# A transformer block on one core: fewer maxima made ahead, another order of token tiles, and where the last transposition stands

## The chip, the cores and the metric

One core of a Trainium2 chip runs the whole program. The metric is the device time of an execution in microseconds (us); the kernel before was run three times, and one further execution was recorded by the profiler.

## The reference

A pre-LayerNorm transformer block in fp32, 2048 tokens, model width 576, 32 heads of 18, and a gated MLP of width 4608. Scale and softmax over all keys, without a mask; LayerNorm without weights.

```python
h  = x + MHA(layernorm(x)) @ wo          # q, k, v = layernorm(x) @ wqkv, 32 heads, Dh = 18
p  = softmax(q @ k.T * Dh**-0.5)         # per head, 2048 x 2048
h2 = h + (gelu(layernorm(h) @ w_gate) * (layernorm(h) @ w_up)) @ w_down
```

The kernel reaches fp32 accuracy by splitting each operand into a high and a low fp16 part.

## The kernel before, in words

**Stages.** (1) LayerNorm, and the products for q, k and v. (2) Attention in 32 blocks `n`: 8 groups of four heads (`g`) times 4 blocks of 512 queries (`qc`); each block runs over 16 tiles of 128 keys (`kt`), one tile a step. (3) The product with wo, token tile by token tile (16 tiles of 128 tokens), with the residual and the statistics of the second LayerNorm. (4) The MLP (line 1246 and on), whose normed rows and their sums are prepared by `rows0` and `rows1`.

**Maxima.** The softmax of a block needs the maximum of each row of scores before its scores are exponentiated. The generator `maxima` makes them: for each block 64 calls of `max_bank`, each four small matmuls (54 rows x 32 columns, a column group each, line 674) into one PSUM bank, and a reduction on DVE (line 687). In one of eight calls ("over") ACT takes the bank instead (line 681), and the last of the eight ("both", line 685) adds this in. A call for head `h` uses the row half `h % 2` of the PE array: rows 0 to 63 or 64 to 127. In each run of eight the heads come as 0, 1, 1, 3, 3, 2, 2, 0.

`max_finish` ends a block: DVE reduces the 64 columns (L698), POOL makes the high and low halves (L701 to L703), SP transposes them by DMA (L705, `mT<-mm`) and copies four parts of `mT` into rows of the query stacks Q (L711, `W<-mT` or `A<-mT`). The first score of the block needs these rows.

**Ahead and beside.** 98 calls of the maxima are made during stage 1, four at a time between the half products of q, k and v (the loop over `i`, line 1369), the rest in the steps of stage 2, eight a pair of steps ("m" in `STEPS`). So the maxima run ahead by 98 calls, and a block's `max_finish` falls into step `kt` = 7 of the block before it. In a step, "S" and "s" are scores and their exponentials on ACT, "w" is `weigh` (the product with V, L765), "f" takes a portion of side work, mostly POOL's: `prepare_wo` in block 2, `split_early` (line 1160) and the sums of `split_matrix` (L1114) from block 28 to 30.

**Late steps.** The maxima end 24 steps before the end of stage 2 (`LAST_MAX`). From there the steps follow `LATE`: in place of the maxima each takes "L", a half token tile of the product with wo (14 matmuls of 288 columns, L335, added to x on DVE at L908). `wo_pairs` goes over tiles 0, 4, 1, 5, 2, 6, 3, 7, then `wo_block(2)` over tiles 8 to 11: 24 halves. After the second tile of each pair POOL makes the reciprocal deviations (`rstd_beside`) of both, and `rows0`, taken in portions by `rows_at`, makes the rows for the MLP, transposed by SP (L996).

**Block outputs.** `out_block(n)` has three parts: in the next block's first step the sums are copied out (L776, L777) and the denominators sent round by DMA (L780); at `kt` = 3 come the reciprocals (POOL L787, DVE L793 from block 28 on; L795, L798); at `kt` = 9 the product (POOL L801 to L803; DVE L805 to L807 from block 29 on), and the copies of the block's rows into X (L822, L826 `X<-nat`) on SP's and POOL's queues. Blocks 28 to 31 are the last head group of the four query blocks, so tokens 0 to 511 (tiles 0 to 3) need block 28's rows, and tiles 4 to 7 block 29's. Block 29's third part comes at `kt` = 8 of block 30, by the exception in line 1413.

**Order.** The instructions of each engine, SP's queue included, stand in the order of the program: what waits holds up what is behind it on the same engine. At the step with `after` == -1 (the last with maxima: `n` = 30, `kt` = 7) SP also gets the load of x tiles 5 to 7 (L1421) and two loads for `wo_block(2)` (L897).

After the loop come `weigh` of the last half, what is left of `fill` (nothing), and the second half; then the MLP.

Of the kernel before, what the change touches and what calls it, by code (L numbers as in the profile page):

```python
# [32 lines left out]
def tile_block(  # L33
# [23 lines left out]
    NT = S // P  # L57
    TB = min(512, S)
    NB = S // TB
    TPB = TB // P  # L60
# [67 lines left out]
    def view(region, off, shape, dtype=None):  # L128

        dtype = dtype or region.dtype  # L130
        v = region if dtype == region.dtype else region.bitcast(dtype)
        size = 4 if dtype == F32 else 2
        n = math.prod(shape)
        assert off % size == 0
        v = v[:, off // size : off // size + n]
        if len(shape) == 2:
            v = v.rearrange("p (a b) -> p a b", b=shape[1])
        elif len(shape) == 3:
            v = v.rearrange("p (a b c) -> p a b c", b=shape[1], c=shape[2])
        return v  # L140
# [188 lines left out]
    def accumulate(dst, pairs, bank=None):  # L329

        xs = []
        for i, (a, b) in enumerate(pairs):
            if i == len(pairs) // 2:
                yield
            m_ = nc.tensor.matmul(dst, a, b, start=(i == 0), stop=(i == len(pairs) - 1))  # L335
            if isinstance(bank, int):
                xs.append(of_triple(m_, (bank,), True))
        if xs:
            wrote((bank,), xs)

    def run(it):
        for _ in it:
            pass
# [8 lines left out]
    def take(it, n=1):  # L352
        for _ in range(n):
            next(it, None)
# [340 lines left out]
    def max_finish(n, mx):  # L695
        g, qc = divmod(n, NB)
        m = small.tile([P, 4, TPB], F32, tag="m", name="m")
        nc.vector.tensor_reduce(m, mx.rearrange("p t h c -> p h t c"), axis=AX.X, op=ALU.max)  # L698
        mm = mms[n % 2]
        hst = mm[:, : 8 * TPB].rearrange("p (h s t) -> p h s t", h=4, s=2)  # L700
        nc.gpsimd.tensor_scalar_mul(m, m, 1 / MSC)  # L701
        nc.gpsimd.tensor_copy(hst[:, :, 0], m)
        nc.gpsimd.tensor_sub(hst[:, :, 1], m, hst[:, :, 0])  # L703
        mT = small.tile([P, 1, P], F16, tag="mT", name="mT")
        nc.sync.dma_start_transpose(mT, mm)  # L705
        for pr in range(2):
            Q = sets[g % 2][pr][0]
            for j in range(2):
                k = (4 * pr + 2 * j) * TPB
                row = 64 * j + R1  # L710
                nc.sync.dma_start(Q[row : row + 2, qc * TB : (qc + 1) * TB],  # L711
                                  mT[k : k + 2 * TPB, 0])
# [117 lines left out]
    NS = NG * NB  # L830
    UPS = TPB * NB
    AHEAD = UPS + 8 * UPS // 16
# [3 lines left out]
    def maxima():  # L836

        for n in range(NS):
            mx = small.tile([P, TPB, 4, NB], F32, tag="mx", name="mx")
            over, both = ("over", "both") if n else ("one", "one")  # L840
            if n:
                nc.gpsimd.memset(mx[:, :, 0, 1::2], LOWEST)
            for u in range(0, UPS, 2):
                t, k = divmod(u, NB)
                for unit in ((over, t, k + 1, 0), ("one", t, k, 1), ("one", t, k + 1, 1), ("one", t, k, 3),
                             ("one", t, k + 1, 3), ("one", t, k, 2), ("one", t, k + 1, 2), (both, t, k, 0)):
                    max_bank(n, mx, *unit, bank=bank_now[0])
                    yield
            max_finish(n, mx)

    oh = view(W, 6 * 2 * S, (NK + 1, D))
    ol = view(W, 6 * 2 * S + 2 * (NK + 1) * D, (NK + 1, D))
# [33 lines left out]
    xbs = [view(A, MAT, (D,)), view(WK, 19968, (D,))]  # L886
# [3 lines left out]

    def wo_tiles(ts, ring_, xbs=xbs):

        by = ts[1] - ts[0]

        def fetch(k):
            if xbs and k < len(ts):
                nc.sync.dma_start(xbs[k % 2], xv[:, ts[k]])  # L897

        fetch(0)
        fetch(1)  # L900
        yield
        for k, t in enumerate(ts):
            for i in range(2):
                ws = slice(i * HALF, (i + 1) * HALF)
                pt = next(ring_)
                run(accumulate(pt[:, :HALF], products(slice(t * P, (t + 1) * P), oh, ol, ws)))
                of_x = xbs[k % 2] if xbs else nat[:, t]
                nc.vector.scalar_tensor_tensor(nat[:, t, ws], pt[:, :HALF], u_o, of_x[:, ws],  # L908
                                               op0=ALU.mult, op1=ALU.add)
                if i == 1:  # L910
                    fetch(k + 2)
                    row_stats(nat[:, t], t)
                    if k % 2:
                        rstd_beside(t - by, 2, 256.0, by)
                        rows_made.update((t - by, t))
                yield
# [4 lines left out]

    def wo_pairs(ring_):

        return wo_tiles([t for i in range(TPB) for t in (i, TPB + i)], ring_, None)


    VP = view(V, 0, (2 * PIECES, TB), F16)
# [428 lines left out]
    mxs = maxima()  # L1356
# [10 lines left out]
    side = iter(())  # L1367
    take(fill, 19)
    for i in range(5 * AHEAD // 4):
        take(mxs, 0 if i % 5 == 4 else 6 if i == 5 * AHEAD // 4 - 2 else 4)  # L1370
        if i == AHEAD // 4:
            raw_loads()
        take(fill, 2 + (i % 6 == 2))
        if i >= AHEAD // 3:
            take(sums)
        if i == 5 * AHEAD // 4 - 6:
            nc.scalar.activation(root, eps, AF.Exp)
            scale_wo()
# [3 lines left out]
    STEPS = [step.split() for step in ("m4 S010 w m2 s25 m3 w s34 f", "m0 S011 m5 w s34 s23 m0 w m5 m2 f")]  # L1382
    halves = deque([None, None])
    LATE = "S010 s22 s33 w L w f".split()
    LAST_MAX = (NS - 1) * NT - 8
    rows_at = {4 * (i + 1) + k: c for i in range(TPB) for k, c in ((1, 2), (3, 3), (4, 3))}
    rows = rows0()
    in_order.enter_context(tc.manual_schedule(engines={EngineType.SP}))
    loads = iter(())
    for n in range(NS):  # L1390
        g, qc = divmod(n, NB)
        late = n > NS - NB
        for kt in range(NT):
            after = n * NT + kt - LAST_MAX
            for step in LATE if after >= 0 else STEPS[kt % 2]:
                if step[0] in "sS":
                    score(n, kt, [int(c) for c in step[1:-1]], int(step[-1]))
                elif step[0] == "m":
                    bank_now[0] = int(step[1])
                    take(mxs)  # L1400
                elif step == "L":
                    take(fill)
                elif step == "w":
                    half_ = halves.popleft()
                    if half_ is not None:
                        weigh(*half_)
                        if half_[1] == NT - 1 and half_[3] == 1:
                            ob = out_block(half_[0], accs)
                            next(ob)
                else:  # L1410
                    take(side)
            halves += [(n, kt, accs, q) for q in range(2)]
            if n and kt in (2 if n == NS - 1 else 3, {NS - 1: 5, NS - 2: 8}.get(n, 9)):
                take(ob)
            if 8 <= n < 13 and kt == 14:
                nc.sync.dma_start(nat[:, n - 8], xv[:, n - 8])
            if after == -1:
                wo_ring = ring([singles[1], quad])
                fill, third = wo_pairs(wo_ring), wo_block(2, wo_ring)
                take(fill)  # L1420
                nc.sync.dma_start(nat[:, 5:8], xv[:, 5:8])  # L1421
                take(third)
                fill = chain(fill, third)
            take(rows, rows_at.get(after, 0))
            if g == 0 and qc == 0 and kt == NT - 1:
                run(fill)
                init_set(sets[1])
            if g + 1 < NG and (qc, kt) == ((1, 2) if g == 0 else (0, 10)):
                loads = load_group(g + 1)
            take(loads)  # L1430
            if g + 1 < NG and qc == 1 and kt == 10:
                steps_made = key_steps(g + 1)
                take(steps_made)
            if g + 1 < NG and qc == 1 and kt == 13:
                run(steps_made)
            if n == 2 and kt == 4:
                side = prepare_wo()
            if n == NS - NB and kt == 0:
                blank_rows()
                loads = matrix_loads(w_gate, 0, nc.gpsimd)  # L1440
                take(loads)
            if n == NS - NB and kt == 2:
                run(loads)
                side = chain(split_early(0, 0, lambda: load_matrix(w_up, 0, nc.gpsimd)), pause(2),
                             split_early(0, 1, lambda: load_matrix(w_gate, 1, nc.gpsimd)),
                             pause(2), until_ready(second))
# [55 lines left out]
    for sc in range(NCH // 2):  # L1502
        c = 2 * sc
# [52 lines left out]
```

## Time and profile before

| | us |
|---|---|
| median of three runs | 2581.53 (2581.3 to 2583.08) |
| the profiled execution | 2580.42 |
| its span, first to last instruction | 2578.6 |
| PE busy | 2545.7 (99%) |
| DVE busy | 1990.8 (77%) |
| ACT busy | 1654.7 (64%) |
| POOL busy | 913.8 (35%) |
| first matmul of the maxima | 103.78 |
| first score | 208.95 |
| end of the maxima (last L698) | 1276.56 |
| MLP begins | 1370.07 |

The rows of the profile have these forms. A timeline row: start in us, duration in us, engine, line, operation, output<-input with shapes, xcount for merged neighbours, and in brackets the idle time before it and what ended it. A row of the chain: start, duration, engine, tile, line. A row of the waits: who waited, for whom, total us, times, longest. A row of stretches: from:to, length, then busy time (and instructions) of PE, PEld, DVE, ACT, POOL, the granted clock of PE, the share of the DMA engines, GB/s. PE is TensorE's matmuls, PEld its weight loads, SPq SP's DMA queue. A busy PE is not PE at its peak.

### The profile page before, as it was taken

The numbers are of one execution on the slowest core, as the hardware profiler recorded it, in microseconds if no ns is written. First come the engines' busy times: TensorE is split into PE (matmuls) and PEld (weight loads), VectorE is DVE, ScalarE is ACT, GpSimd is POOL, SyncE is SP. The second block draws the span as 40 slices with busy tenths as digits, with TensorE's granted clock in tenths as the row PEclk, the third lists the DMA queues.
The fourth block names the chain that finished last, engine by engine and source line by source line (L and its number), as shares of the span: only waits on it lengthen the run. The fifth ranks groups of instructions, "written<-read, shape, count | busy, mean of one in ns | idle before, by whom it ended". The sixth has DMA issues, their size and how long they took to land.

```text
span 2578.6 us, 95994 instructions
## 1 busy us (share of the span) xinstructions
PE 2545.7 (99%) x41245; PEld 1472.2 (57%) x41245; DVE 1990.8 (77%) x3891; ACT 1654.7 (64%) x2723; POOL 913.8 (35%) x1299
## 2 busy tenths in 40 slices
PE   8999999999999999999989999999999999999999
PEld 4645555555555555555555555555555555555555
DVE  7478999999999999999856674757575756565653
ACT  7437999999999999999855433334343424333332
POOL 4301644343434343446846332323231323232221
PEclk9999999999999999999999999999999999999999
DMA  8620111021202010111133410101010101010110
GB/s 220 155 72 28 48 37 33 17 59 28 52 19 49 21 46 21 41 25 30 39 80 90 93 44 14 51 12 52 13 35 30 34 30 35 30 34 30 35 56 37
DMA packets 177601, 120.98 MB, mean 47 GB/s; under 512 B 94188, under 2 KB 154548, under 8 KB 177174
## 3 DMA queue, kind: packets, MB, share of 16 engines
q1 hardware_dynamic: 163378, 95.92, 14.0%
q0 software_dynamic: 13664, 18.91, 3.0%
q8 instruction: 322, 5.28, 0.9%
q14 instruction: 105, 0.86, 0.1%
q10 hardware_dynamic: 132, 0.01, 0.0%
HBM read 80.05 MB, written 15.01 MB: 37 GB/s over the span
## 4 chain that ended last, share of the span: by engine, by line
PE 74%; DVE 18%; issue 5%; POOL 2%; DMA 1%; ACT 1%; SPq 0%; DVEq 0%; ACTq 0%; POOLq 0%
PE more L1246 15%; PE bank L1246 15%; DVE mx L687 13%; PE bank L335 10%; PE bank L765 9%; PE more L335 8%; PE triple L674 4%; DVE nat L685 3%; PE bank L674 3%; PE triple L742 2%; PE triple L335 2%; PE bank L742 2%; PE quad L335 2%; PE quad L674 1%; DMA A<-qk_hi 0%
## 5 line engine op out<-in xcount | busy, mean ns | idle before, releaser
L765 PE MATMUL bank<-WK,V 64*32 64x256 f32 x16384 | 761.1, 379 | 0.1
L751 ACT ACTIVATE WK<-triple 128x1024 f32<-128x1024 f32 x512 | 539.9, 1054 | 43.7 <-PE triple L742 42.3
L687 DVE TENSOR_REDUCE mx<-triple 128x1 f32<-128x512 f32 x731 | 499.6, 683 | 1.1 <-PE quad L674 0.3
L753 ACT ACTIVATE WK<-bank 128x512 f32<-128x512 f32 x756 | 434.1, 617 | 3.7 <-PE bank L742 0.3
L687 DVE TENSOR_REDUCE mx<-bank 128x1 f32<-128x512 f32 x577 | 387.4, 680 | 23.1 <-PE bank L674 22.2
L1246 PEld LDWEIGHTS <-W 128*128 128x128 f16 x2394 | 234.2, 98 | 278.4 <-issue 0.2
L335 PEld LDWEIGHTS <-WK 128*128 128x128 f16 x3456 | 338.2, 98 | 88.3
L765 PEld LDWEIGHTS bank<-WK,V 64*32 64x32 f32 x16384 | 351.0, 106 | 44.8 <-DVE nat L777 7.6
L674 PEld LDWEIGHTS <-W 54*32 54x32 f16 x4096 | 143.1, 89 | 169.9 <-issue 107.1
L335 PE MATMUL more<-W,WK 128*128 128x288 f16 x1728 | 235.2, 286 | 0.0
L335 PE MATMUL bank<-W,WK 128*128 128x288 f16 x1728 | 235.2, 286 | 0.0
L674 PEld LDWEIGHTS <-A 54*32 54x32 f16 x4096 | 136.8, 89 | 169.1 <-issue 109.0
L787 POOL TENSOR_TENSOR rp<-rc,minus_one 128x4 f32<-128x4 f32 x112 | 111.6, 1010 | 339.3 <-DMA rc<-nat 339.3
L1246 PE MATMUL more<-X,W 128*128 128x512 f16 x792 | 223.8, 379 | 0.0
L1114 POOL TENSOR_TENSOR A<-A 128x384 f32<-128x384 f32 x136 | 138.9, 1042 | 199.6 <-DMA A<-in_B_w_up_dram 115.2
L674 PE MATMUL triple<-W 54*32 54x512 f16 x2048 | 203.0, 384 | 2.8 <-DVE mx L687 1.3
L1246 PE MATMUL more<-V,W 128*128 128x512 f16 x720 | 202.4, 379 | 0.0
L1260 POOL TENSOR_TENSOR WK<-tmp,WK 128x512 f16<-128x512 f32 x73 | 88.2, 1208 | 308.0 <-ACT WK L1257 307.9
L674 PE MATMUL triple<-A 54*32 54x512 f16 x1852 | 184.2, 385 | 2.0 <-ACT WK L751 0.5
L685 DVE CUSTOM_DVE_ANT_0 nat<-triple,nat 128x512 f32<-128x512 f32 x244 | 165.6, 679 | 0.9 <-PE triple L674 0.9
L687 DVE TENSOR_REDUCE mx<-quad 128x1 f32<-128x512 f32 x244 | 165.7, 679 | 0.2 <-PE quad L674 0.2
L1264 ACT COPY tmp<-bank 128x512 f32<-128x512 f32 x36 | 21.0, 583 | 222.3 <-PE bank L1246 220.7
(363 smaller groups left out, 4676.5 us busy)
## 6 DMA issues: line engine op xcount, KB each, us to landing
A<-in_B_w_down_dram SPq DMA_DIRECT2D x8, 1152.0 KB
nat<-rc SPq DMA_DIRECT2D x128, 64.0 KB
A<-in_B_w_gate_dram SPq DMA_DIRECT2D x64, 128.0 KB
A<-in_B_w_up_dram SPq DMA_DIRECT2D x64, 128.0 KB
qk_hi<-tmp SPq DMA_DIRECT2D x36, 128.0 KB
qk_lo<-tmp SPq DMA_DIRECT2D x36, 128.0 KB
out_dram<-nat SPq DMA_DIRECT2D x16, 288.0 KB
nat<-in_A_x_dram SPq DMA_DIRECT2D x3, 1152.0 KB
```

The source lines that it names most:

```text
L335: m_ = nc.tensor.matmul(dst, a, b, start=(i == 0), stop=(i == len(pairs) - 1))
L674: mm = [nc.tensor.matmul(pm[c : c + CT, :TB], Q[r, q0 + c : q0 + c + CT], keys, start=True, stop=True) for c in range(0, P, CT)]
L685: x_ = nc.vector.tensor_tensor_reduce(row, pm[:, :TB], row, 1.0, LOWEST, ALU.add, ALU.max, dst)
L687: x_ = nc.vector.tensor_reduce(dst, pm[:, :TB], axis=AX.X, op=ALU.max)
L742: mm.append(nc.tensor.matmul(pS[c : c + CT, :TB], K[r, k0 : k0 + CT], Q[r, qc * TB : (qc + 1) * TB], start=True, stop=True))
L751: act = nc.scalar.activation(pe, triple[:, bank : bank + 2], AF.Exp, scale=ex_reg)
L753: act = nc.scalar.activation(pe[:, heads[0] % 2], bank_at(bank)[:, :TB], AF.Exp, scale=ex_reg)
L765: nc.tensor.matmul(acc[CT * c : CT * c + CT, :QH], Vg[n // NB][ks, v : v + CT], pes[(2 * kt + q) % NPE][ks, j, qh * QH : (qh + 1) * QH], s ...
L787: nc.gpsimd.tensor_tensor(rc[:, c : c + 4], den[:, c : c + 4], minus_one.to_broadcast([P, 4]), op=ALU.pow)
L1114: op(W8[:, d], W8[:, a], W8[:, b])
L1246: nc.tensor.matmul(bank, w, x_, start=start and i == 0, stop=i == len(mm) - 1, skip_group_check=not start)
L1260: nc.gpsimd.tensor_sub(hl[:, 2 * i + j], v, hh[:, 2 * i + j])
```

## The change

- Of the maxima, 90 calls instead of 98 are made in stage 1: four at a time up to `i` = 26, two at 27, none at 28 and 29. In these the heads of a run of eight come as 0, 1, 1, 2, 3, 2, 3, 0, so that the row halves alternate.
- So every `max_finish` falls two steps later, into `kt` = 9 of the block before, ahead of that step's third part of `out_block`. The maxima end two steps later, at `n` = 30, `kt` = 9; there are 22 late steps, and two half tiles (tile 11) are taken by `run(fill)` between the two last calls of `weigh`.
- For the last block, `max_finish` pauses eight times between POOL's part and the transposition. Block 29's third part moves from `kt` = 8 to 9, the same step, and `run(mxs)` issues the last transposition and its four copies behind it.
- The token tiles come as 0, 1, 4, 5, 2, 6, 3, 7; `rstd_beside` is called after each tile from 4 on; the steps at which `rows0` is taken follow.

```diff
@@ max_finish
         nc.gpsimd.tensor_sub(hst[:, :, 1], m, hst[:, :, 0])
+        if n == NS - 1:
+            yield from [None] * 8
         mT = small.tile([P, 1, P], F16, tag="mT", name="mT")
@@ maxima
-                for unit in ((over, t, k + 1, 0), ("one", t, k, 1), ("one", t, k + 1, 1), ("one", t, k, 3),
-                             ("one", t, k + 1, 3), ("one", t, k, 2), ("one", t, k + 1, 2), (both, t, k, 0)):
+                order = ((over, k + 1, 0), ("one", k, 1), ("one", k + 1, 1), ("one", k, 3),
+                         ("one", k + 1, 3), ("one", k, 2), ("one", k + 1, 2), (both, k, 0))
+                for kind, kc, h in [order[i] for i in (0, 1, 2, 5, 3, 6, 4, 7)] if n * UPS + u < AHEAD - 2 else order:
+                    unit = kind, t, kc, h
                     max_bank(n, mx, *unit, bank=bank_now[0])
                     yield
-            max_finish(n, mx)
+            yield from max_finish(n, mx)
@@ wo_tiles
-        by = ts[1] - ts[0]
+        by = 1 if xbs else TPB
...
-                    if k % 2:
+                    if k % 2 if xbs else t >= TPB:
                         rstd_beside(t - by, 2, 256.0, by)
@@ wo_pairs
-        return wo_tiles([t for i in range(TPB) for t in (i, TPB + i)], ring_, None)
+        return wo_tiles([0, 1, TPB, TPB + 1, 2, TPB + 2, 3, TPB + 3], ring_, None)
@@ stage 1
     for i in range(5 * AHEAD // 4):
-        take(mxs, 0 if i % 5 == 4 else 6 if i == 5 * AHEAD // 4 - 2 else 4)
+        take(mxs, 0 if i % 5 == 4 else 4 if i < 27 else 2 if i == 27 else 0)
@@ stage 2
-    LAST_MAX = (NS - 1) * NT - 8
-    rows_at = {4 * (i + 1) + k: c for i in range(TPB) for k, c in ((1, 2), (3, 3), (4, 3))}
+    LAST_MAX = (NS - 1) * NT - 6
+    rows_at = {7: 2, 8: 3, 9: 3, 10: 2, 11: 3, 12: 3, 13: 2, 15: 3, 16: 3, 17: 2, 19: 3, 20: 3}
...
-            if n and kt in (2 if n == NS - 1 else 3, {NS - 1: 5, NS - 2: 8}.get(n, 9)):
+            if n and kt in (2 if n == NS - 1 else 3, {NS - 1: 5, NS - 2: 9}.get(n, 9)):
                 take(ob)
+            if after == -1:
+                run(mxs)
```

## The prediction

> **What bounds the kernel now.** I read first the page, then the busy times in stretches, then the chain of waits and the timelines around the one stretch in which TensorE is idle.
>
> ```profile
> span 2578.6 us, 95994 instructions
> PE 2545.7 (99%) x41245; PEld 1472.2 (57%) x41245; DVE 1990.8 (77%) x3891; ACT 1654.7 (64%) x2723; POOL 913.8 (35%) x1299
> ```
>
> TensorE is bound nearly everywhere, so a gain must be idle PE time, or PE work. The stretches (us; busy time of each engine; granted clock; DMA share; GB/s):
>
> ```profile
> 107.30:143.30 36.00, 36.00 (x383) 22.46 (x383) 28.63 (x50) 20.43 (x68) 10.91 (x16) 1.00 0.55 129
> 143.30:196.40 53.10, 52.81 (x378) 21.66 (x375) 40.71 (x78) 12.09 (x21) 1.48 (x5) 1.00 0.25 82
> 216.07:1276.50 1060.43, 1055.66 (x31092) 614.05 (x31078) 1056.60 (x2014) 1056.43 (x1731) 470.02 (x750) 1.00 0.14 35
> 1283.08:1302.66 19.58, 9.09 (x133) 4.76 (x125) 2.19 (x8) 4.00 (x6) 0.92 (x2) 0.65 0.27 86
> 1320.92:1368.68 47.76, 47.76 (x891) 30.38 (x896) 32.80 (x87) 28.73 (x44) 29.44 (x59) 1.00 0.62 118
> ```
>
> Before 196 us (maxima beside products) PE is full and DVE is not. In the long middle, with maxima in every step, DVE is as full as PE. In the late steps PE alone is full, except from 1283 to 1303, where it works 9.09 of 19.58 us. Who it waits for there (engine, line, releaser: us, times, longest), and the SP queue at that place:
>
> ```profile
> PE bank L335 <- DMA X<-nat: 10.5, 1, 10.5
> ```
> ```profile
> 1282.56 1.12 SPq L705 DMA_TRANSPOSE mT<-mm  x1
> 1285.51 2.70 SPq L711 DMA_DIRECT2D W<-mT  x4
> ...
> 1289.81 5.07 SPq L822 DMA_DIRECT2D X<-nat  x6
> ```
>
> The second token tile of the order 0, 4, 1, 5 needs block 29's rows (X<-nat). The copies are issued last, behind the last transposition, its four copies and loads of x (lines 1421 and 897, between the two). The transposition itself was late; the chain has POOL's sums of a weight matrix before it:
>
> ```profile
> 1277.75 2.91 POOL A L1114 x3
> ```
>
> It also gives the last copy of rows before PE goes on, issue included, and what a late step costs:
>
> ```profile
> 1293.26 2.51 DMA X<-nat
> ```
> ```profile
> 1302.86 0.41 PE triple L742 x12
> 1303.30 0.43 PE bank L765 x16
> 1303.73 1.82 PE bank L335 x14
> ```
> ```profile
> 1307.01 1.82 PE quad L335 x14
> ```
>
> A late step is 3.28 us (1303.73 to 1307.01), 1.82 of it the half token tile. The stretch 1283.08 to 1302.66 holds two steps and took 19.58, so the stall costs 19.58 - 2 x 3.28 = 13.0 us: 10.5 of waiting, the rest slow matmuls at the lower clock.
>
> **The change, part by part.**
>
> *The stall: tile order (edits of `wo_tiles` and `wo_pairs`), rows ahead of the transposition (the pause in `max_finish`, `run(mxs)` after `take(ob)`).* DVE around the place, with two marks one pair of steps apart:
>
> ```profile
> 1271.48 0.68 DVE L685 CUSTOM_DVE_ANT_0 nat<-triple,nat 128x512 f32<-128x512 f32 x1
> 1275.76 0.68 DVE L685 CUSTOM_DVE_ANT_0 nat<-triple,nat 128x512 f32<-128x512 f32 x1
> 1276.56 0.22 DVE L698 TENSOR_REDUCE m<-mx 128x16 f32<-128x64 f32 x1
> 1279.97 1.24 DVE L805 TENSOR_TENSOR nat<-nat 128x512 f32<-128x512 f32 x1
> 1281.76 0.69 DVE L807 TENSOR_TENSOR nat<-nat 128x512 f16<-128x512 f32 x1
> ```
>
> A pair of steps with maxima is 4.28 us. Two more such steps put the last L698 and the start of the late steps at 1276.5 + 4.3 = 1280.8 (on the time scale of before). L805 to L807 (2.5 us) then follow L698 at once: rows ready at 1283.5. SP is free (its next work is theirs) and issues six copies in 5.07: 1288.6; the last lands at 1287.8 + 2.51 = 1290.3. POOL's own two copies follow the POOL sums of the maxima, which now start with L698, since POOL's backlog L1114 ends at 1280.7. Tiles 0 and 1 need block 28 alone; tile 4 is now the fifth half tile and starts at 1280.8 + 4 x 3.28 + 0.9 (1302.86 to 1303.73) = 1294.8, 4.5 us after the landing. So the wait of the PE goes: -13.0, bounds -13.3 (clock also undisturbed later) and -10 (a few us of it left).
>
> What is late next is the transposition, now behind the six copies: issue 1288.6, first copy 2.95 later as before (1282.56 to 1285.51), 1291.5, four copies 2.70 = 1294.2, and about 1.8 to land (the X copy took 2.51 with 0.8 of issue): 1296. Block 31's first score waits for it and comes with the seventh late step, 1280.8 + 6 x 3.28 = 1300.5. Margin 4.5 us, cost 0. The loads of x queue behind it (1295 to 1296) and tile 5 adds x in that same step, at about 1303.4; so 7 us are left for them. Cost 0, up to 2 if a margin is missed.
>
> *Two steps more with maxima, two late steps less, two half tiles behind the loop.* +4.28 - 2 x 3.28 + 2 x 1.82 = +1.36. The half tiles are not hidden: PE is full up to the end of the loop (47.76 of 47.76), so there is no gap that they could fill. The rows of the pairs 0 and 4, 1 and 5 are taken two or three steps after their later tile (sixth and eighth late step, taken from the eighth and eleventh on), as before; the last portion comes in the second last step, with 3.28 + 1.82 x 2 behind it, 3 us less than before, and the first products of the next stage need the earlier transpositions alone.
>
> *Eight maxima less ahead.* The end of the first stage on PE:
>
> ```profile
> 195.63 0.83 PE L674 MATMUL bank<-A 54*32 54x512 f16 x12
> 196.40 3.19 PE L335 MATMUL quad<-X,W 128*128 128x512 f16 x14
> 199.52 0.84 PE L674 MATMUL bank<-A 54*32 54x512 f16 x16
> ...
> 202.57 3.20 PE L335 MATMUL triple<-X,W 128*128 128x512 f16 x14
> ```
>
> The takes of 4 become 2 at 195.6 and none at 199.5. All from 199.52 to 202.57 goes, 3.05, with the PE's wait for DVE in it; of the group at 195.62, 0.77 long (to 196.40), half goes, 0.4. Sum -3.45. Lower bound: 8 maxima at 0.77 / 4 = 1.5, if what follows then waits for something else.
>
> *Alternating row halves.* A group of four maxima (16 matmuls) in the chain:
>
> ```profile
> 120.32 0.77 PE bank L674 x16
> 121.09 1.82 PE triple L335 x14
> ```
>
> In the late step above, the 16 score matmuls, whose heads alternate between the row halves, took 0.44 (1302.86 to 1303.30): two rounds of 0.22, two row halves side by side in each. The order before has halves 0,1,1,1 and 1,0,0,0, three rounds, 0.66 and 0.11 for the changes from and to full matmuls: 0.77, as measured. The new one, 0,1,1,0 and 1,0,1,0, has two: -0.22 a group. Of 22 groups the first waits for a DMA, and four are paced by DVE:
>
> ```profile
> 148.30 2.47 DVE L687 TENSOR_REDUCE mx<-bank 128x1 f32<-128x512 f32 x4
> 152.20 2.47 DVE L687 TENSOR_REDUCE mx<-bank 128x1 f32<-128x512 f32 x4
> ```
>
> There DVE works 3.9 us a round (2.47 and two other operations) and has no gap to give. 17 x 0.22 = -3.74. Bounds: 0, if DVE paces all, and 22 x (0.77 - 0.44) = -7.3. A loss is excluded: the same matmuls go to the same four banks in turn.
>
> The Trainium skill, page "TensorEngine Tiling (Array Packing)", section Performance Considerations (PSUM Bottleneck), speaks against this part: tiles that run side by side speed up TensorE but not the emptying of PSUM, which can become the bound. By it the part is worth 0 and the gain 3.7 us less. The trace agrees with it in the four groups above, and not on the mean (DVE busy 28.63 of 36 and 40.71 of 53 us).
>
> *The transposition of every block two steps later.* A step is 4.28 / 2 = 2.14, so each L698 comes 4.3 us nearer to the score that needs it. An ordinary block, and block 3, where POOL also splits wo:
>
> ```profile
> 369.07 0.26 POOL L701 TENSOR_SCALAR m<-m 128x16 f32<-128x16 f32 x1 [8.17 <-DVE m L698]
> 372.24 2.77 SPq L711 DMA_DIRECT2D W<-mT  x4
> ```
> ```profile
> 298.77 0.22 DVE m L698
> ```
> ```profile
> 304.51 0.25 POOL L701 TENSOR_SCALAR m<-m 128x16 f32<-128x16 f32 x1
> 305.36 1.74 POOL L866 TENSOR_SCALAR nat<-nat,p_s_wo 128x576 f32<-128x576 f32 x1
> 309.18 1.73 POOL L866 TENSOR_SCALAR nat<-nat,p_s_wo 128x576 f32<-128x576 f32 x1
> ```
> ```profile
> 307.65 2.72 SPq L711 DMA_DIRECT2D A<-mT  x4
> 316.36 0.41 PE L742 MATMUL triple<-A 56*32 56x512 f16 x8
> ```
>
> L698 to first score was 316.36 - 298.77 = 17.6 and becomes 13.3. Ordinary: L701 to the last copy's issue 375.0 - 369.1 = 5.9, with 0.3 before and 1.8 after it 8.0: hidden, 5.3 to spare. Block 3: POOL now passes two more portions of wo first (309.18 - 305.36 = 3.8), so L701 comes at 308.3, the last issue at 308.3 + 310.37 - 304.51 = 314.2, landed 316.0, against 316.36. I take 0.3, for the little that is left; bounds 0 and 2. POOL's queue: in the step the sums of the maxima stay ahead of block rows, as before. SP's: the block's row copies go out up to 4 us later behind the four copies, and the loads of the next group behind them; the rows are read in the late steps only, the loads a block later.
>
> **The sum.** -13.0 + 1.36 - 3.45 - 3.74 + 0.3 = -18.5 from the profiled execution, 2580.42 us (its span 2578.6 and 1.8 around it, which the change doesn't touch): 2561.9. The median of the runs (2581.53) stands 1.1 above it: 2563.0.
>
> **The rivals.**
>
> (a) *DVE paces the first stage.* The alternation brings 0 and the maxima taken away their 1.5: -13.0 + 1.36 - 1.5 + 0.3 = -12.8, 2568.7. For it the two DVE rows; against it the full PE of the stretches, where DVE is free for a fifth of the time. Chance 0.16. (The rule of the Trainium skill above describes this case.)
>
> (b) *The change doesn't do what it says: the wait stays, or moves to block 31's score.* If the rows still land behind the transposition, or the queue behind them makes the score wait as long, only the rest remains: 1.36 - 3.45 - 3.74 + 0.3 = -5.5, 2576. It takes 4.5 us more between L698 and the last copy; for it the transposition of before, 6 us after its L698; against it that this delay was POOL's backlog, over by then, and that 2.5 + 5.1 of the new order hide it. 0.08.
>
> (c) *Slower: the 13.3 us don't do for the ordinary blocks.* Place: first score of each of 31 blocks; price: the landing's excess over 13.3. It decides against the change from 18.5 / 31 = 0.6 us a block, a landing at 13.9 where 8.0 is worked out: the chain would have to grow by three quarters. With 1 us each: 2563 + 31 = 2594. 0.04.
>
> **How the numbers follow.** Forecast 0.70 (own range 2559 to 2567), (a) 0.16, (b) 0.08, (c) 0.04, unnamed 0.02. Within 0.2% (5.2 us) is about what a measurement of this kernel can't tell from no change. Low end: the alternation's -7.3 instead of -3.74, 2559.4, taken as 2558.5. High end: (a) with 2 us of a margin missed, 2571. Faster by over 0.2%: forecast, (a) and most of (b), 0.92; same 0.04; slower 0.04.
>
> **What would show it.** Stall: no PE wait for X<-nat over 0.5 us at about 1285 to 1300, clock 1.00 there, copies X<-nat of block 29 ahead of the last transposition, block 31's first score without a wait for mT. Two half tiles between the two last weighings, each 1.82. First stage: 16 matmuls of a group in about 0.55, main loop begun some 7 us earlier. Block 3: a PE wait for mT below 1 us, none in other blocks. Wrong it would be if a DMA wait on mT shows at several block starts, if PE waits for DVE (L687) in many groups of the first stage, or if the late steps stall at another place.

## The result, and the profile after

| | before | after |
|---|---|---|
| median, us (lowest to highest) | 2580.44 (2578.22 to 2583.08, 6 runs) | 2564.56 (2563.48 to 2566.1, 6 runs) |
| the profiled execution | 2580.42 | 2564.0 |
| its span | 2578.6 | 2562.2 |

After to before 0.9941, 95% interval 0.9931 to 0.9952: 15.9 us less between the medians, 16.4 between the profiled executions. The sum had said 18.5.

The page's head, and the stretches after (from the second group of maxima to 143.30, where the prediction's row also ends; to the first score; to the first late step; to the MLP):

```profile
span 2562.2 us, 96008 instructions
PE 2538.5 (99%) x41245; PEld 1470.1 (57%) x41245; DVE 1996.4 (78%) x3891; ACT 1654.0 (65%) x2723; POOL 912.7 (36%) x1299
```
```profile
105.70:143.30 37.60, 37.60 (x393) 22.44 (x393) 29.00 (x51) 20.97 (x69) 10.55 (x16) 1.00 0.53 127
143.30:202.20 58.90, 58.26 (x409) 24.05 (x407) 43.85 (x85) 13.10 (x22) 1.48 (x5) 1.00 0.26 86
202.20:1273.57 1071.37, 1065.75 (x31323) 621.47 (x31322) 1065.26 (x2030) 1065.22 (x1745) 470.06 (x751) 1.00 0.14 35
1273.57:1353.20 79.63, 77.32 (x1424) 48.82 (x1423) 53.94 (x125) 44.52 (x68) 45.58 (x92) 1.00 0.41 94
```

In the table "first stage" runs from the first full matmul behind the first group of maxima to the first score.

| us | before | after | difference | the sum's terms |
|---|---|---|---|---|
| up to there | 105.48 | 103.88 | -1.60 | 0 |
| first stage | 103.47 | 98.32 | -5.15 | -3.45 - 3.74 = -7.19 |
| first score to first late step | 1067.56 | 1071.37 | +3.81 | +4.28 + 0.3 = +4.58 |
| late steps to MLP | 93.56 | 79.63 | -13.93 | -13.0 - 6.56 + 3.64 = -15.92 |
| MLP | 1208.53 | 1209.00 | +0.47 | 0 |
| span | 2578.6 | 2562.2 | -16.40 | -18.53 |

The first and last rows, which the change doesn't touch, vary as much between traces of kernels alike there (start 103.9 to 107.4, MLP 1208.5 to 1209.25). The part from first score to first late step varies by 1 to 2 us; over nine traces with 90 maxima ahead it averages 1071.6, over four with 98 1066.5: +5.1. A part of this is PE's clock: in 8 of these 13 traces it falls to 0.50 for some 3 us, from about 3 us behind the first score on, in 5 it doesn't (last section). Like with like it is 1067.56 to 1071.83 with the fall (+4.3; one trace and the mean of seven) and 1066.12 to 1070.86 without it (+4.7; means of three and of two), around the 4.58 of the sum.

SP's queue at the place of the stall, and all waits of PE from 1270 to 1360:

```profile
1277.80 5.00 SPq L824 DMA_DIRECT2D X<-nat  x6
1282.90 1.13 SPq L707 DMA_TRANSPOSE mT<-mm  x1
1285.14 2.81 SPq L713 DMA_DIRECT2D W<-mT  x4
```
```profile
PE bank L335 <- DVE nat L912: 1.6, 1, 1.6
PE quad L335 <- DVE nat L912: 0.6, 1, 0.6
PE triple L744 <- DVE mx L685: 0.4, 1, 0.4
```

The six rows' copies go out first, the transposition right behind them at 1282.90, and no wait for X<-nat or for mT is left. Two waits for DVE are new. The late steps follow each other at 3.28, and the two half tiles behind the loop cost what a half tile costs:

```profile
1277.94 1.82 PE quad L335 x14
1281.22 1.82 PE bank L335 x14
```
```profile
1349.07 1.89 PE L335 MATMUL bank<-W,X 128*128 128x288 f16 x14
1350.80 1.88 PE L335 MATMUL quad<-W,X 128*128 128x288 f16 x14
```

In the first stage the groups of four maxima, all 0.77 to 0.78 before (but the first, three of 0.96 to 1.18 and the last), now alternate. The chain there, and DVE:

```profile
118.23 0.94 PE bank L674 x16
...
120.99 0.57 PE bank L674 x14
...
123.38 0.92 PE bank L674 x16
```
```profile
116.24 4.87 DVE L687 TENSOR_REDUCE mx<-bank 128x1 f32<-128x512 f32 x8 [1.61 <-PE bank L674]
121.37 4.88 DVE L687 TENSOR_REDUCE mx<-bank 128x1 f32<-128x512 f32 x8 [0.26 <-PE bank L674]
129.07 2.48 DVE L687 TENSOR_REDUCE mx<-bank 128x1 f32<-128x512 f32 x4 [2.83 <-PE bank L674]
```

```profile
PE bank L674 <- DVE mx L687: 0.4, 2, 0.2
```

In these rounds every second group takes 0.37 us longer than the 0.57 of the one between, while the waits of PE from 100 to 205 (the last fence) list only two of 0.2 us for DVE's maxima: the delay lies inside groups that count as busy. A full PE (37.60 of 37.60) does not show that DVE is not the pace.

### The profile page after: what moved, and what is told of

The parts are those of the page before. It is cut to its first block, busy times and chain, and to the rows that moved or that the text cites. A ratio compares the mean times of both kernels' runs of the same rounds, so it can differ in the third digit from the quotient of the medians.

```text
span 2562.2 us, 96008 instructions
## 1 busy us (share of the span) xinstructions
PE 2538.5 (99%) x41245; PEld 1470.1 (57%) x41245; DVE 1996.4 (78%) x3891; ACT 1654.0 (65%) x2723; POOL 912.7 (36%) x1299
## 4 chain that ended last, share of the span: by engine, by line
PE 69%; DVE 23%; issue 6%; DMA 1%; POOL 1%; ACT 0%; SPq 0%; DVEq 0%; ACTq 0%; POOLq 0%
DVE mx L687 17%; PE more L1250 15%; PE bank L1250 15%; PE bank L335 10%; PE more L335 8%; PE bank L767 7%; DVE nat L685 4%; PE triple L674 3%; PE bank L674 2%; PE triple L335 2%; PE triple L744 2%; PE quad L335 2%; PE bank L744 1%; PE quad L674 1%; DVE st L222 0%
## 5 line engine op out<-in xcount | busy, mean ns | idle before, releaser
L685 DVE CUSTOM_DVE_ANT_0 nat<-triple,nat 128x512 f32<-128x512 f32 x245 | 166.0, 677 | 0.8 <-PE triple L674 0.8
```

Source lines behind the costliest of these rows:

```text
L685: x_ = nc.vector.tensor_tensor_reduce(row, pm[:, :TB], row, 1.0, LOWEST, ALU.add, ALU.max, dst)
```

## The experiments

Medians and ratios are each against runs of the kernel before on the same chip. Stage lengths are from the traces, as in the table above. The first stage of the kernels with 90 ahead came out at 98.31 or 98.32 in four traces in which it is the same, so tenths of a us count there. With 98 ahead it was 103.46 or 103.47 in three traces and 105.11 in the fourth ("rows ahead alone"), in which the clock fell near its end (last section).

**Heads as before.** The changed kernel, without the alternation.

```diff
-                for kind, kc, h in [order[i] for i in (0, 1, 2, 5, 3, 6, 4, 7)] if n * UPS + u < AHEAD - 2 else order:
+                for kind, kc, h in order:
```

> The changed kernel with the heads of a run of eight in the order of before (0, 1, 1, 3, 3, 2, 2, 0) in stage 1. Theory A, DVE paces most of stage 1, so that the alternation brought only what the trace of the changed kernel suggests: 1.6 us slower, 2566.2, groups of 16 matmuls at 0.77 and few waits, from the end of the first group to the first score 99.9 us instead of 98.25. Rival B, the prediction's term (17 groups x 0.22 = 3.7): 2568.3, 102 us.

Measured: 2567.07, ratio 0.9946 (0.9931 to 0.9961); first stage 99.87, all groups 0.77 or 0.78 again but the first, the last and the same three. So the alternation gave 99.87 - 98.32 = 1.55 us, not 3.74. Against the 103.47 of before, the eight maxima taken away gave 3.60 (3.50 by the sum of the groups, 20.91 to 17.41); against the one trace with 98 ahead in which the clock fell it would be 5.2.

**Half reads.** The changed kernel, in which the reductions of the first stage read half of each bank. It leaves out the maxima over the other half of these columns.

```diff
-            x_ = nc.vector.tensor_reduce(dst, pm[:, :TB], axis=AX.X, op=ALU.max)
+            x_ = nc.vector.tensor_reduce(dst, pm[:, : TB if n > 1 or bank is not None else TB // 2], axis=AX.X, op=ALU.max)
```

> The changed kernel, where DVE's maxima of stage 1 read half of each bank (256 of 512 columns; the maxima of block 0 and part of block 1 leave out the other half of the keys). Theory A, DVE paces stage 1: with DVE relieved every group of 16 matmuls takes 0.56 (in the changed kernel every second one takes 0.92 to 0.94), and the time from the end of the first group to the first score falls from 98.25 by about 10 x 0.37 and the two longer waits, to some 94 us. Rival B, the long groups wait for something on PE's side (weight loads, changes of tile mode): they stay at 0.92, 98 us.

Measured: 2562.62, ratio 0.9928 (0.9908 to 0.9948); a reduction takes 0.415 for 0.68, the first stage 95.14, and the groups that had alternated all take 0.56:

```profile
117.52 0.56 PE bank L674 x16
...
119.89 0.56 PE bank L674 x16
```

One group of 1.18 at 175 us stays; it waits for other work of DVE. With DVE out of the way two row halves do work side by side at 0.22 us a round, as the prediction's price has it. DVE alone held 3.2 us back.

**More maxima through ACT.** The changed kernel, with the pairs "over" and "both" also for the last two token tiles of block 0, so that ACT empties a bank of each eight there too.

```diff
-            over, both = ("over", "both") if n else ("one", "one")
+            t0 = 0 if n else 2
...
+                over, both = ("over", "both") if t >= t0 else ("one", "one")
```

> The changed kernel, where the second half of block 0's maxima also lets ACT take one bank of eight (over and both, as in all other blocks). Theory A, DVE paces stage 1: four reductions of 0.64 us less on DVE in stage 1, up to 2 us gained, 2563 to 2564.6, long groups fewer in the second half of block 0. Rival B, PE paces: no difference, 2564.6. If the key steps land too late, a wait of PE there, slower.

Measured: 2565.63, ratio 0.9943 (0.9926 to 0.9959); first stage 98.46, no gain. The groups (without the first) fell from 15.8 to 14.9 us in all, but the keys that an "over" call reads have not landed:

```profile
130.24 0.40 PE L674 MATMUL bank<-nat,A 54*32 54x512 f16 x4 [1.03 <-DMA nat<-kd]
```

The relief was taken back by one DMA wait of 1.03.

**Takes spread evenly** (on the version "rows apart" below). In the changed kernel four rounds of five take four maxima and the fifth none; here all thirty take 4 and 2 in turn, 90 as well.

```diff
-        take(mxs, 0 if i % 5 == 4 else 4 if i < 27 else 2 if i == 27 else 0)
+        take(mxs, 2 if i % 2 else 4)
```

> The version e4_rows_apart, with the 90 units of maxima of the first stage taken 4, 2, 4, 2 over all 30 rounds instead of 4, 4, 4, 4, 0. Theory A (in the changed kernel every second group of maxima waits for VectorE, 0.92 to 1.22 us instead of 0.56, because four rounds in five ask VectorE for more than it can do in a round, while its mean load fits): 15 groups of four at 0.56 and 15 of two at about 0.34, 13.5 us instead of 15.9, the first stage 98.3 - 2.4 = 95.9 us, the kernel about 2560.0 (0.9920 of before). Rival B (VectorE has no slack even on the mean, with its other work in this stage): groups of 0.9 stay, first stage 98.3 and the kernel 2562.4. Rival C (each group costs a fixed time for the change between tiled and whole matmuls, more than 0.1 us): seven more groups cost over 2 us, 2562 or more, but with no PE wait for VectorE in the groups.

Measured: 2561.96, ratio 0.9923 (0.9909 to 0.9936); first stage 96.20 for 98.32. The chain and DVE:

```profile
119.24 0.34 PE bank L674 x8
...
121.40 0.56 PE bank L674 x16
...
123.78 0.34 PE bank L674 x8
```
```profile
117.25 3.68 DVE L687 TENSOR_REDUCE mx<-bank 128x1 f32<-128x512 f32 x6 [0.87 <-PE bank L674]
```

DVE now idles 0.87 us in a pair of rounds, and a group costs its matmuls: 0.56 for 16, 0.34 for 8, which is 0.22 a round and 0.12 around it. Theory A holds, with 2.1 us for the 2.4 expected. B falls with the groups of 0.9 gone. C, by which the changes take the gain, falls with these 2.1 us, but a part of it is there: seven more groups with 0.12 each, and 0.65 more in the time between the groups, which by themselves fell by 2.8 (15.8 to 13.1). The median alone, 2561.96, does not decide between 2560.0, 2562.4 and 2562.

**The old heads, evenly taken.** The version above without the alternation, with the edit of the first experiment.

> The version e10_even_takes with the maxima of the first stage in the order of heads of the kernel before (0, 1, 1, 3, 3, 2, 2, 0). Taken by 4 and 2, this order needs 18 rounds of 0.22 us of matmuls in 8 groups where the alternating one needs 12: 67.5 for 45 over the 90 units. Theory A (0.22 us a round was the right price of the alternation, and VectorE's pace in the bunched groups hid it; evenly taken, nothing hides it): first stage 96.2 + 22.5 x 0.22 = 101.1 us, kernel about 2566.5, so that the alternation is worth 4.9 us here for the 1.55 us between the changed kernel and e1_heads_as_before. Rival B (the alternation is worth 1.5 to 2 us in any case, since VectorE's work takes the rest): first stage about 97.9 us, kernel 2563.5.

Measured: 2564.72, ratio 0.9930 (0.9914 to 0.9947); first stage 100.45, groups 0.77, 0.34, 0.77, 0.55 in turn. The alternation is worth 100.45 - 96.20 = 4.25 us here, 0.7 less than Theory A's 4.9 but far from B's 1.6: its price a round was right, and the bunched takes hid most of it.

**Rows apart.** The changed kernel, with the first portion of `rows0` a step earlier and the third part of block 30's output two steps later in block 31.

```diff
-    rows_at = {7: 2, 8: 3, 9: 3, ...}
+    rows_at = {6: 2, 8: 3, 9: 3, ...}
...
-            if n and kt in (2 if n == NS - 1 else 3, {NS - 1: 5, NS - 2: 9}.get(n, 9)):
+            if n and kt in (2 if n == NS - 1 else 3, {NS - 1: 7, NS - 2: 9}.get(n, 9)):
```

> The changed kernel with the first portion of rows one late step earlier (6 for 7) and block 30's third part at kt = 7 of the last block for 5, so that it no longer meets two portions of three. Theory A, the two waits of PE for DVE's L912 in the late steps (0.64 and 1.60 us) come from these meetings: both go, 2562.3. Rival B, DVE is full there and the waits come back at other late steps: 2564.6. Rival C, block 30's rows come too late for tile 8: a wait for X<-nat, up to 3 us, 2565 to 2568.

Measured: 2562.39, ratio 0.9933 (0.9920 to 0.9947); late steps 77.29 for 79.63, and of the three waits shown above only the 0.4 us for L685 is left. The 2.3 us are those of the two waits for L912 (1.6 and 0.64). Their cause, in the changed kernel's timeline (DVE, then PE):

```profile
1306.84 0.76 DVE L972 CAST V<-nat 128x1152 f16<-128x1152 f32 x1 [3.01 <-POOL nat L963]
1311.21 0.51 DVE L912 SCALAR_TENSOR_TENSOR nat<-quad,u_o,nat 128x288 f32<-128x288 f32 x1
...
1317.12 0.91 DVE L807 TENSOR_TENSOR nat<-nat 128x512 f32<-128x512 f32 x1
...
1320.11 0.75 DVE L972 CAST tmp<-V 128x1152 f16<-128x1152 f32 x1
1322.71 0.51 DVE L912 SCALAR_TENSOR_TENSOR nat<-bank,u_o,nat 128x288 f32<-128x288 f32 x1
```
```profile
1311.77 1.88 PE L335 MATMUL quad<-W,X 128*128 128x288 f16 x14 [0.64 <-DVE nat L912]
1323.27 1.88 PE L335 MATMUL bank<-W,X 128*128 128x288 f16 x14 [1.60 <-DVE nat L912]
```

A cut of the rows waits 3.01 us for POOL's portion of one step before, and block 30's product stands ahead of the next cut. Behind them comes L912, which frees the PSUM bank of the next half tile. The two shifts were made together: that both waits go is measured, which shift took which is read from these rows.

**The parts of the stall.** Four kernels take the three edits apart: the changed kernel with the old tile order (0, 4, 1, 5); the changed kernel with the transposition (`run(mxs)`) ahead of the rows (`take(ob)`); the kernel before with the rows ahead of the transposition alone; and the kernel before with the tile order alone.

```diff
# tiles as before
+        return wo_tiles([0, TPB, 1, TPB + 1, 2, TPB + 2, 3, TPB + 3], ring_, None)
# transposition first
+            if after == -1:
+                run(mxs)
             if n and kt in (2 if n == NS - 1 else 3, {NS - 1: 5, NS - 2: 9}.get(n, 9)):
                 take(ob)
# rows ahead alone: the pause in max_finish and run(mxs) behind take(ob) added to before, and
-            if n and kt in (2 if n == NS - 1 else 3, {NS - 1: 5, NS - 2: 8}.get(n, 9)):
+            if n and kt in (2 if n == NS - 1 else 3, {NS - 1: 5, NS - 2: 7}.get(n, 9)):
# tile order alone: the edits of wo_tiles, wo_pairs and rows_at added to before
```

> The changed kernel with the token tiles in the order of before (0, 4, 1, 5). Theory A, that the rows are issued ahead of the transposition removes most of the stall by itself: the last copy lands at about 1284.5, tile 4 (third half tile) needs it at its tenth matmul, 1282.3: a wait of 2.2 us, 2566.8. Rival B, the tile order is what removed the stall: a wait of 10 us and a lower clock, 2575 or more.

> The changed kernel with the last transposition issued ahead of block 29's rows (run(mxs) ahead of take(ob)), tile order as changed. Theory A, the tile order removes most of the stall by itself: transposition at 1278.5, its copies 1281.4 to 1284.2, the rows to 1289.2, landed 1290.9, needed by tile 4's tenth matmul at 1288.9: a wait of 2.0 us, 2566.6. Rival B, the place of the transposition decides: a wait of 8 us or more, 2573. Without any wait: 2564.6.

> The kernel before with block 29's rows (at kt = 7) ahead of the last transposition alone (98 maxima ahead, tiles 0, 4, 1, 5). DVE's three operations end 4 us after L698 as in the changed kernel, the copies 5 us later, the last lands 1.7 after: 1276.6 + 4.1 + 5.0 + 1.7 = 1287.4; tile 4's tenth matmul at 1285.3. Theory A: a wait of 2 us, the clock stays, 13.0 - 2 = 11 us gained, 2569.5. Rival B, the transposition now is late for block 31's score: a wait at 1304, less gained.

> The kernel before with the new tile order and its portions of rows alone (98 maxima ahead, transposition ahead of block 29's rows). Tile 4 starts at 1276.5 + 4 x 3.28 + 1.0 = 1290.6, its tenth matmul at 1291.8; the rows land at 1295.8. Theory A, the stall becomes that difference: 4 us, clock lower for a step, 13.0 - 5 = 8 us gained, 2572.5. Rival B, order alone does nothing, 2580.4; rival C, it takes away all, 2567.

| | median | ratio (95%) | late steps | waits for X<-nat |
|---|---|---|---|---|
| tiles as before | 2565.87 | 0.9944 (0.9929 to 0.9959) | 80.57 | 0.77 |
| transposition first | 2566.02 | 0.9942 (0.9927 to 0.9958) | 80.78 | 0.98 |
| rows ahead alone | 2568.94 | 0.9952 (0.9936 to 0.9969) | 81.54 | 0.83 |
| tile order alone | 2582.0 | 1.0004 (0.9994 to 1.0014) | 95.48 | 4.69 and 4.73 |

Each of the two edits is almost enough in the changed kernel: without one or the other 0.8 to 1.0 us of the wait come back, half or less of the 2.2 and 2.0 that were expected. Alone on the kernel before they differ: the rows ahead take 93.56 - 81.54 = 12.0 us off the late steps, and the tile order, of which 8 us were expected, makes them 1.9 longer. It cut the 10.5 us to 4.69, but a second wait for rows appeared at 1342, those of block 30. Either the order makes it or the shifted `rows_at` does, which was made for maxima that end two steps later. So that was tried apart: the tile order alone, with the portions one to two steps earlier.

```diff
-    rows_at = {7: 2, 8: 3, 9: 3, 10: 2, 11: 3, ...}
+    rows_at = {6: 2, 7: 3, 8: 3, 9: 2, 11: 3, ...}
```

> The kernel before with the change's tile order alone, the rows of block 29 behind the last transposition as before, and the row portions one to two steps earlier than in e6_tile_order_alone (steps 6, 7, 8, 9 for 7, 8, 9, 10). Theory A (the order alone moves the half tile that needs block 29's rows by two late steps, 6.6 us, and the second wait of e6 came only from the row portions' shift against block 30's output): one PE wait of about 4.7 us for X<-nat stays, with slow matmuls behind it, the second goes; the late steps take some 6.5 us less than in e6 (95.5), about 89, and the kernel 2575 us, 0.9978 of before. Rival B (the second wait belongs to the order itself, since the SP queue is behind whatever the row portions do): two waits of 4.7 us again, 2582 us.

Measured: 2575.81, ratio 0.9983 (0.9974 to 0.9992); late steps 89.23. The waits of PE there:

```profile
PE bank L335 <- DMA X<-nat: 4.9, 1, 4.9
PE bank L765 <- DVE nat L777: 1.3, 1, 1.3
```

One wait is left, the second is gone: the rows' schedule had made it, as Theory A has it. The tile order by itself is worth 93.56 - 89.23 = 4.3 us, with a new wait of 1.3 for L777 in it.

## Why the prediction was right, and where its sizes were off

**The stall: right.** Rows issued in 5.00 us (5.07 predicted), the transposition behind them at 1282.90, 5.1 later than the first row copy; neither the fifth half tile nor block 31's score waits. One premise failed, at no cost: POOL's sums of a weight matrix were not over by then. They moved with the steps, and POOL's part of the maxima came 3.7 us behind the last L698 (1273.62 to 1277.31), as against 4.2 before. The transposition would have been late by that again, but it waited behind the rows' copies in any case, and those need little of POOL. Both edits were counted as one part. The runs show that they overlap: the rows ahead of the transposition alone would have taken 12.0 of the 13.0.

What DVE needs for the rows was 2.5 us by the row of before, and took 3.9, with POOL's sums beside them until 1277.2:

```profile
1273.82 1.41 DVE L807 TENSOR_TENSOR nat<-nat 128x512 f32<-128x512 f32 x1
1275.32 1.05 DVE L808 CAST nat<-nat 128x512 f16<-128x512 f32 x1
1276.40 1.37 DVE L809 TENSOR_TENSOR nat<-nat 128x512 f16<-128x512 f32 x1
```
```profile
1273.67 3.55 POOL L1118 TENSOR_TENSOR A<-A 128x384 f32<-128x384 f32 x3
1277.31 0.57 POOL L701 TENSOR_SCALAR m<-m 128x16 f32<-128x16 f32 x1
```

The margin of 4.5 us covered this.

**Two steps more with maxima, two late steps less, two half tiles behind: right in the parts.** Late steps of 3.28, as in the sum; half tiles of 1.89 and 1.88 that start 1.73 apart, for its 1.82; the steps with maxima at +3.8 in the two profiled executions, and +4.3 or +4.7 between traces with the same clock behind the first score, for its 4.28.

**Eight maxima less: -3.45 predicted, -3.6 measured**, against the 103.46 or 103.47 that three of four traces with 98 ahead have in the first stage.

**Alternating row halves: the step that was mis-sized, -3.74 for -1.55.** The price of a round was right (0.22). Wrong was the count of 17 groups that DVE would let go faster. The argument was a mean: DVE busy for 28.63 of 36 us, a fifth of the time free. That fifth was the fifth round of the loop, which takes no maxima. In the others, up to 137 us, DVE had nothing left, and the timeline of before showed it:

```profile
118.10 10.26 DVE L687 TENSOR_REDUCE mx<-bank 128x1 f32<-128x512 f32 x16 [1.82 <-PE bank L674]
131.05 1.29 DVE L687 TENSOR_REDUCE mx<-bank 128x1 f32<-128x512 f32 x2 [2.68 <-PE bank L674]
```

Sixteen reductions without a gap in 10.26 are 2.565 a round, against 0.77 + 1.82 = 2.59 on PE. The slack was 0.03 us a round, not the 0.22 that the step took. Group by group, against the first experiment, the 1.55 is made up so: 0.47 from the eleven groups up to 137 us (0.56, 0.94, 0.57, 0.92 in a run of four rounds, for four times 0.77), nothing from the four up to 158, and 1.08 from five groups behind 163, which stand 3.7 us or more apart, with products of 512 columns between them. One of these five in the first experiment, and in the changed kernel:

```profile
165.34 0.77 PE bank L674 x16
```
```profile
163.32 0.56 PE bank L674 x16
```

So five groups gained the full 0.21 or so, not 17. Groups that wait for DVE were one of the prediction's own signs of being wrong; it came, though the list of waits hid it. Rival (a) named this mechanism and took the alternation's gain as 0 (and the maxima taken away as 1.5, where 3.6 came). The Trainium skill, page "TensorEngine Tiling (Array Packing)", section Performance Considerations (PSUM Bottleneck), says that tiling speeds up TensorE and not the emptying of PSUM, which may then become the bottleneck. The half reads agree with it (3.2 us back when a read takes 0.415), and so do the even takes. Its advice to let ACT empty banks as well relieved the groups by about 1 us here, and met the landing of the keys.

**Late rows: a step costed at nothing, worth 2.24.** The prediction said that the rows' portions follow their tiles "as before" and looked only at their end. It named no cover for DVE, though DVE's L912 stands in order behind them; the spacing between POOL's portion, DVE's cut and block 30's product is what changed. The "another place" at which late steps might stall is this one.

**Every transposition two steps later: no cost seen.** Block 3, bounded from 0 to 2 and taken as 0.3:

```profile
296.02 0.22 DVE L698 TENSOR_REDUCE m<-mx 128x16 f32<-128x64 f32 x1
301.71 0.25 POOL L701 TENSOR_SCALAR m<-m 128x16 f32<-128x16 f32 x1
304.84 2.72 SPq L713 DMA_DIRECT2D A<-mT  x4
309.07 0.41 PE L744 MATMUL triple<-A 56*32 56x512 f16 x8
```

L698 to the block's first score (the last row) is 13.05 us, for the 13.3 worked out. POOL reached L701 5.7 behind L698, for the 5.3 that the sum has (308.3, with L698 4.3 later than 298.77). The last copy is issued by 307.56, 1.5 before the score, so the margin is about as thin as forecast: with the prediction's estimate of 1.8 to land there is none. PE has no wait for mT in any block, so the 0.3 did not show.

In all, 1.55 for 3.74 and 2.24 for 0 made the sum's gain 4.4 us too large; the other rows of the table gave 2.3 back, 1.60 of it the start, which the change doesn't touch. That is luck, and so is the rest of the closeness: the median, forecast as 2563.0, came out only 1.6 above, because that of before, over six runs, is 1.1 below the one that the forecast started from; the gain between the medians, 15.9, is 2.6 short of 18.5.

## What to carry to other kernels

A mean busy share over a loop with uneven rounds says nothing of the rounds in which the work is: divide an unbroken run of the second engine's instructions by its count, and set that against the first engine's pitch, before pricing a speed-up of the first. Where both are near, spread the work evenly first; here that raised the worth of the same reordering from 1.55 to 4.25 us. And when steps are shifted against each other, follow the in-order engines between them too, not only the last portion: here the shift cost 2.24 us through DVE instructions that came to stand ahead of L912.

The version with rows apart and even takes stands at 0.9923 (0.9909 to 0.9936) of before, the change at 0.9941 (0.9931 to 0.9952); the intervals overlap, but the traces show the 2.3 and 2.1 us in their stages. The even takes alone are not told apart by the medians (2562.39 without them, 2561.96 with them, on two chips).

## What the runs showed of the hardware

In the late steps the clock fell with the longer waits alone. Behind one of 0.77 us the granted clock was 1.00 (behind the 1.60 for L912 too), behind one of 4.88 it was 0.50 for 3.1 us (stretches of "tiles as before", and of the order alone with earlier rows):

```profile
1282.80:1284.40 1.60, 0.83 (x14) 0.52 (x21) 0.00 (x0) 0.28 (x1) 0.00 (x0) 1.00 0.09 23
```
```profile
1290.03:1294.90 4.87, 0.00 (x0) 0.02 (x1) 0.00 (x0) 0.26 (x1) 0.00 (x0) 0.79 0.56 193
1294.90:1298.00 3.10, 3.09 (x45) 1.50 (x53) 0.52 (x1) 0.15 (x1) 0.00 (x0) 0.50 0.02 6
```

So the waits that were cut to below a us cost their own length only. But the length of a wait does not decide alone. In the first 3.6 us from the first score PE is busy for 2.06 us and waits for 1.07 and 0.47 us, in each of the 13 traces; behind that the clock falls to 0.50 in 8 of them and stays at 1.00 in 5. The next 3.1 us, in the changed kernel and in "tiles as before":

```profile
205.80:208.90 3.10, 3.10 (x68) 2.26 (x71) 1.81 (x4) 2.31 (x4) 0.00 (x0) 0.54 0.01 3
```
```profile
207.33:210.43 3.10, 3.10 (x105) 2.08 (x107) 3.02 (x6) 3.10 (x6) 0.00 (x0) 1.00 0.01 3
```

In "rows ahead alone" it fell earlier, behind waits of 1.28 and 0.20 us for DVE at the last group of the first stage, which the three other traces with 98 ahead have too, without a fall:

```profile
202.20:205.30 3.10, 3.06 (x11) 0.99 (x10) 1.79 (x4) 0.48 (x1) 0.00 (x0) 0.52 0.04 11
```

That is the 105.11 for 103.46 of its first stage; with 90 ahead this group, and its wait, are gone. The Trainium skill, page "TensorE: Matmul & The Clock Gate", section Part 1, gives an idle window of about 3.4 us, running freely, as what brings the clock down. The 4.88 in the late steps agrees with it; the falls behind the first score come without any idle time over 1.07 us. What decides there stays open.

DVE's three operations of the rows took 2.36 us in all before, with POOL's sums of 384 columns beside the first of them and sums of 16 beside the others, and 3.83 after, with the wide sums beside nearly all of it. That POOL slows them was not tried apart. The Trainium skill, page "GPSIMD Engine Reference", section 1 (Specifications), names a contention of POOL with DVE operations that have two inputs in SBUF or run in a 2-port mode; the middle operation, a cast with one input, also grew, from 0.43 to 1.05, and no run shows in which mode it ran.
